# Moving the first product's operands to the same places modulo 256 bytes as the second product's

## The chip, the cores and the metric

One core of a Trainium2 chip runs the kernel. The metric is the device time of one execution in microseconds (us). Three runs of the kernel before gave 1517.08, 1517.21 and 1517.23 us. SBUF, the on-chip memory, has 128 partitions; each tile takes the same byte range in every partition, and "place" below means the address within a partition.

## The reference

Four batches of 12480 tokens of width 128 go through an attention that passes through 32 inducing points, and then all 49920 tokens go through a two-layer network of inner width 2048:

```python
h = mab(I, x)                       # I: 32 inducing vectors, softmax over the 12480 tokens
y = mab(x, h)                       # each token attends to the 32 rows of h
def mab(q, kv):
    s = scale * (q @ kv.transpose(0, 2, 1))
    a = np.exp(s - s.max(-1, keepdims=True))
    a /= a.sum(-1, keepdims=True) + 1e-09
    return a @ kv
t = y @ w_in                        # (49920, 128) @ (128, 2048)
out = (t * sigmoid(1.702 * t)) @ w_out
```

The results are float32. The two weight matrices arrive as 64-bit floats and are decoded on the chip.

## The kernel before

The attention's last product and the first layer are joined: `w_in` is multiplied by `h` ahead of time, so that a block of 512 tokens needs, in place of its 128 attention outputs, only its 32 attention weights. Each operand is split into a rounded part and a remainder, and the parts are stacked on the 128 partitions. Per block of 512 tokens there are 16 chunks of 128 inner columns. They are handled two at a time, as a *group*.

- `hidden(i)` issues the two **first products** of group i: weights `hw` (128x128), moving columns `st` (512 tokens), result in a two-bank PSUM tile `ph`. Two such tiles take turns. (A shorter last block of each batch uses the tile `left` in place of `st`.)
- `first(i)` then lets ScalarE make `g` (the gated value) from `ph`, ScalarE or VectorE make `hi` (its rounded part), and VectorE make `lo = g - hi`.
- `second(i, c)` issues three **second products** for each chunk c: weights `wl` with moving `hi`, weights `wh` with moving `lo`, weights `wh` with moving `hi`. The 48 of one block add up in one PSUM tile `pso`, of which two take turns; ScalarE copies it out to `ob` at the end.

So a group is eight matmuls of 512 columns. TensorE's order is written out in advance: the loop at the end of the kernel puts in the two first products of a later group when its own cost model says that a `ph` tile is free, else the next second products. Matmuls of the next batch's attention (`pa`, from `xt`, `xn`, `indT_sb`, `hT`) are put in between by the same means. Each engine then runs its list in order, held by semaphores.

Both operands of a rounded matmul are read from SBUF. `by_lines` makes the 512 moving columns be read as four passes; in each pass 4 neighbouring columns (16 bytes) are taken out of every 16 (64 bytes):

```python
LINES = (4, 4)
ASIDE = 4
def by_lines(ap):
    return ap.rearrange("p (n s i) -> p s n i", s=LINES[0], i=LINES[1])
```

The weights of a matmul are 128 neighbouring float32 (512 bytes). `aside` places `hw`, `wh` and `wl` 4 elements (16 bytes) behind the start of their tile. Where each tile starts follows from the order in which the pools are opened and from the sizes of the small tiles in the pools between them (`SMALL` says which small tile goes to which pool).

Of the kernel before, what the change touches and what calls it, by code (L numbers as in the profile page):

```python
# [9 lines left out]
F32 = mybir.dt.float32  # L10
# [10 lines left out]
P = 128  # L21
# [44 lines left out]
FB = 6  # L66
LINES = (4, 4)
ASIDE = 4
SMALL = {"m2": "psm1", "less": "psm2", "rs2": "psm4", "row": "psm4", "mx": "psm4", "den": "psm5", "rs": "psm5", "sm": "psm6"}
WINDOW = 100.0  # L70
CHAIN = 200.0
CALM = 0
# [179 lines left out]
def set_attention_then_moe(ctx: ExitStack, tc, xT, x, indT, w_in, w_out, outT):  # L252
# [75 lines left out]
    const = ctx.enter_context(tc.tile_pool(name="const", bufs=1))  # L328
# [3 lines left out]
    pools = {}  # L332

    def pool_of(name, bufs=1):
        pools[name] = ctx.enter_context(tc.tile_pool(name=name, bufs=bufs))
        return pools[name]
# [10 lines left out]
    pool_of("psm5", 2)  # L347
    pool_of("pwl")
    pool_of("psm6", 3)
    pools["psm5"].tile([P, 8], F32, tag="aside", name="aside", bufs=1)  # L350

    def small(shape, tag, name, **k):
        return pools[SMALL.get(tag, "psm3")].tile(shape, F32, tag=tag, name=name, **k)

# [21 lines left out]
    rep2 = rep.rearrange("p g m -> p (g m)")  # L376
    mine = const.tile([P, M], F32, name="mine")
    dve.tensor_scalar(mine, rep[:, 0, :], -scale, None, op0=ALU.mult)
    ones = const.tile([1, 2], F32, name="ones")
    one, warm = ones[:, 0:1], ones[:, 1:2]  # L380
    dve.memset(one, 1.0)
    act.activation(warm, one, AF.Exp)
# [1235 lines left out]
```

## Time and profile before

| | before |
|---|---|
| median of 3 runs | 1517.21 us |
| time of the profiled execution | 1517.26 us |
| its span, first to last instruction | 1515.5 us |
| TensorE matmuls busy | 1507.8 us (99%) |
| ScalarE busy | 1343.5 us (89%) |
| VectorE busy | 1300.5 us (86%) |
[...]

The span is what the trace covers; 1.8 us of the execution's time lie around it. "PE" is TensorE's matmuls and "PEld" its weight loads, "DVE" VectorE, "ACT" ScalarE. Matmuls overlap in the pipeline, so a matmul's shown duration is longer than the time from its start to the next one's start, which this document calls a *step*.

### The profile page before, as it was taken

To read this page: it belongs to the slowest core of one execution; us is meant where nothing else is said; L and a number is where in the kernel's file an instruction comes from. 1 tells how busy PE (TensorE), PEld (TensorE's weight loads), DVE (VectorE), ACT (ScalarE), POOL (GpSimd) and SP (SyncE) were. 2 spreads that over 40 slices of the span, in tenths; PEclk is the share of its full clock that TensorE was granted. 3 is DMA by queue.
4 is the path that set the end of the run, shared out by engine and by line. 5 is a ranking of instruction groups with operands and counts; after the bars stand their busy time and mean duration, and the time that the engine had idled before them with its cause. 6 is when DMAs were issued, how large, how long until landed. Compare 5 with 4: busy or idle time off the path is not lost.

```text
span 1515.5 us, 21743 instructions
## 1 busy us (share of the span) xinstructions
PE 1507.8 (99%) x7736; PEld 1226.8 (81%) x7736; DVE 1300.5 (86%) x1512; ACT 1343.5 (89%) x1549; POOL 0.7 (0%) x6
## 2 busy tenths in 40 slices
PE   9999999999999999999999999999999999999999
PEld 6588878887888888887887888888788888888888
DVE  7988888889888887889889888778988898888996
ACT  4899999998999888899999898989899998988884
POOL 0000000000000000000000000000000000000000
PEclk9999999999999999999999999999999999999999
DMA  8210167713051115933123110871301101101100
GB/s 339 64 62 23 42 217 125 200 56 105 30 211 43 34 32 99 187 105 103 44 98 136 41 49 15 160 205 55 100 23 40 49 25 39 49 22 42 49 24 23
DMA packets 83849, 127.53 MB, mean 84 GB/s; under 512 B 12320, under 2 KB 50848, under 8 KB 77856
## 3 DMA queue, kind: packets, MB, share of 16 engines
q1 hardware_dynamic: 83600, 126.05, 29.5%
q8 instruction: 63, 1.03, 0.3%
q14 instruction: 42, 0.34, 0.1%
q10 hardware_dynamic: 144, 0.10, 0.0%
HBM read 72.11 MB, written 25.56 MB: 64 GB/s over the span
## 4 chain that ended last, share of the span: by engine, by line
PE 98%; DVE 1%; DMA 1%; ACT 0%; issue 0%; SPq 0%
PE pso L185 69%; PE ph L185 24%; PE pa L185 4%; PE h L185 0%; PE spun L1299 0%; DMA xt<-in_xT 0%; ACT g L185 0%; DMA hw<-tl 0%; DVE e L185 0%; DVE sm L185 0%; ACT s L185 0%; DVE m L185 0%; DVE two L185 0%; DVE aT L185 0%; DVE hw L185 0%
## 5 line engine op out<-in xcount | busy, mean ns | idle before, releaser
L185 DVE TENSOR_TENSOR lo<-g,hi 128x1024 fp32r<-128x1024 f32 x776 | 937.7, 1216 | 117.8 <-ACT hi L185 104.9
L185 ACT ACTIVATE g<-ph 128x1024 f32<-128x1024 f32 (+1 forms) x784 | 814.6, 1045 | 135.3 <-PE ph L185 68.0
L185 PE MATMUL pso<-hi,wh 128*128 128x512 f32 (+1 forms) x1552 | 593.8, 383 | 0.0
L185 PE MATMUL pso<-hi,wl 128*128 128x512 f32 (+1 forms) x1552 | 590.2, 380 | 0.0
L185 PE MATMUL pso<-lo,wh 128*128 128x512 f32 (+1 forms) x1552 | 589.6, 380 | 0.0
L185 ACT ACTIVATE hi<-ph 128x1024 fp32r<-128x1024 f32 (+1 forms) x493 | 515.0, 1045 | 0.0
L185 PE MATMUL ph<-st,hw 128*128 128x512 f32 x1536 | 477.2, 394 | 1.3 <-ACT g L185 0.9
L185 PEld LDWEIGHTS ph<-st,hw 128*128 128x128 f32 x1536 | 284.7, 187 | 72.2 <-issue 9.6
L185 PEld LDWEIGHTS pso<-hi,wl 128*128 128x128 f32 x1552 | 291.0, 187 | 59.7 <-issue 2.5
L185 PEld LDWEIGHTS pso<-lo,wh 128*128 128x128 f32 x1552 | 291.0, 187 | 57.6
L185 PEld LDWEIGHTS pso<-hi,wh 128*128 128x128 f32 x1552 | 291.2, 188 | 49.9
L185 DVE CAST hi<-g 128x1024 fp32r<-128x1024 f32 (+1 forms) x283 | 193.6, 684 | 71.4 <-ACT g L185 71.0
L185 ACT COPY ob<-pso 128x512 f32<-128x512 f32 (+1 forms) x98 | 60.6, 619 | 9.9 <-PE pso L185 9.7
L185 ACT ACT_TABLE_LOAD x26 | 33.4, 1283 | 1.2 <-PEq L1608 0.7
L185 PE MATMUL pa<-xt,indT_sb 128*32 128x512 f32 x200 | 24.9, 600 | 0.6 <-DVE aT L185 0.6
L185 ACT ACTIVATE s<-s,nmx 128x512 f32<-128x512 f32 (+1 forms) x27 | 17.8, 660 | 4.2 <-DVE nmx L185 4.2
L185 PE MATMUL pa<-xt,hT 128*32 128x512 f32 (+1 forms) x176 | 21.3, 593 | 0.0
L185 DVE TENSOR_TENSOR e<-e,sm 128x512 f32<-128x512 f32 (+3 forms) x29 | 17.8, 613 | 1.0
L185 DVE TENSOR_REDUCE m<-e 128x16 f32<-128x512 f32 (+2 forms) x28 | 17.3, 618 | 1.0
L185 DVE STREAM_TRANSPOSE aT<-s 128x512 f32<-128x512 f32 (+1 forms) x28 | 17.9, 641 | 0.2
L185 DVE TENSOR_REDUCE sm<-e 128x16 f32<-128x512 f32 (+3 forms) x29 | 17.3, 597 | 0.4 <-ACT e L185 0.4
L185 DVE TENSOR_TENSOR e<-e,m 128x512 f32<-128x512 f32 (+2 forms) x28 | 17.3, 616 | 0.0
(120 smaller groups left out, 356.9 us busy)
## 6 DMA issues: line engine op xcount, KB each, us to landing
xt<-in_xT SPq DMA_DIRECT2D x44, 1024.0 KB, 7.9
out_T<-ob SPq DMA_DIRECT2D x96, 256.0 KB, 2.0
xn<-in_x SPq DMA_DIRECT2D x72, 256.0 KB, 7.3
st<-ahT SPq DMA_DIRECT2D x184, 64.0 KB, 2.0
st<-alT SPq DMA_DIRECT2D x184, 64.0 KB, 2.0
raw<-in_w_in SPq DMA_DIRECT2D x4, 512.0 KB, 10.8
xf<-in_x SPq DMA_DIRECT2D x2, 1024.0 KB, 17.3
raw<-in_w_out SPq DMA_DIRECT2D x4, 512.0 KB, 15.3
```

The source lines that it names most:

```text
L185: return f(*a, **k)
```

## The change

No instruction is added, removed or put elsewhere: the lists of all five engines are the same, row for row. Some small tiles go to other pools and one (`ones`) leaves the pool of constants. Because of that everything between the constants and the pool `psm3` starts 32 bytes lower, and what lies behind it stays.

```diff
-SMALL = {"m2": "psm1", "less": "psm2", "rs2": "psm4", "row": "psm4", "mx": "psm4", "den": "psm5", "rs": "psm5", "sm": "psm6"}
+SMALL = {"m2": "psm1", "less": "psm2", "den": "psm4", "rs": "psm4", "mx1": "psm5", "nmx": "psm5", "rs1": "psm5", "sm": "psm6"}
...
-    pools["psm5"].tile([P, 8], F32, tag="aside", name="aside", bufs=1)
+    pools["psm4"].tile([P, 8], F32, tag="aside", name="aside", bufs=1)
...
-    ones = const.tile([1, 2], F32, name="ones")
+    ones = pools["psm5"].tile([1, 2], F32, tag="ones", name="ones", bufs=1)
```

The places that follow, modulo 256 bytes, are the same for all buffers of a name (a chunk's 128 weights are 512 bytes, so all chunks of a tile share one place):

| matmul | weights before | moving before | weights after | moving after |
|---|---|---|---|---|
| first product `ph<-st,hw` | 48 | 0 | 16 | 224 |
| second `pso<-hi,wl` | 16 | 224 | 16 | 224 |
| second `pso<-lo,wh` | 16 | 224 | 16 | 224 |
| second `pso<-hi,wh` | 16 | 224 | 16 | 224 |

Within each matmul the weights lie 48 bytes ahead of its own moving columns (the columns 208 bytes behind the weights), before and after. What differs is a pair of neighbours: the weights of the *next* matmul are loaded while the columns of this one stream. From a second product into a first one the weights being loaded lie 80 bytes (48 - 224 + 256) ahead of the columns being streamed, from a first into a second one 16 (16 - 0); after the change it is 48 everywhere. `left`, `xt`, `xn`, `aT`, the score tiles and `w_in_all` go down by 32 bytes too, while `indT_sb`, `hT`, `hi`, `lo` and `g` stay.

## Rows read from the trace of the kernel before

**Rows 1.** Page: engines' busy time; the chain that ended last, by engine and line.
```profile
span 1515.5 us, 21743 instructions
PE 1507.8 (99%) x7736; PEld 1226.8 (81%) x7736; DVE 1300.5 (86%) x1512; ACT 1343.5 (89%) x1549; POOL 0.7 (0%) x6
...
PE 98%; DVE 1%; DMA 1%; ACT 0%; issue 0%; SPq 0%
```

**Rows 2.** Groups of TensorE: names, shape, count | busy us, mean ns | idle before.
```profile
L185 PE MATMUL pso<-hi,wh 128*128 128x512 f32 (+1 forms) x1552 | 593.8, 383 | 0.0
L185 PE MATMUL pso<-hi,wl 128*128 128x512 f32 (+1 forms) x1552 | 590.2, 380 | 0.0
L185 PE MATMUL pso<-lo,wh 128*128 128x512 f32 (+1 forms) x1552 | 589.6, 380 | 0.0
L185 PE MATMUL ph<-st,hw 128*128 128x512 f32 x1536 | 477.2, 394 | 1.3 <-ACT g L185 0.9 <-DMA hw<-tl 0.4
```

**Rows 3.** Timeline of TensorE from 1359.72 us: start us, duration us, engine, matmul.
```profile
1359.72 0.38 PE L185 MATMUL pso<-hi,wl 128*128 128x512 f32 x1
...
1360.82 0.38 PE L185 MATMUL pso<-hi,wh 128*128 128x512 f32 x1
1361.04 0.38 PE L185 MATMUL pso<-hi,wl 128*128 128x512 f32 x1
...
1361.48 0.39 PE L185 MATMUL pso<-hi,wh 128*128 128x512 f32 x1
1361.71 0.62 PE L185 MATMUL ph<-st,hw 128*128 128x512 f32 x2
1362.17 0.38 PE L185 MATMUL pso<-hi,wl 128*128 128x512 f32 x1
```

**Rows 4.** Timeline of ScalarE around 1361 us.
```profile
1360.59 1.10 ACT L185 ACTIVATE g<-ph 128x1024 f32<-128x1024 f32 x1
1361.49 0.68 ACT L185 COPY ob<-pso 128x512 f32<-128x512 f32 x1
```

**Rows 5.** Timeline of TensorE: first and last of 28 first-product pairs.
```profile
1425.42 0.62 PE L185 MATMUL ph<-st,hw 128*128 128x512 f32 x2
...
1473.66 0.62 PE L185 MATMUL ph<-st,hw 128*128 128x512 f32 x2
```

**Rows 6.** Timeline of TensorE at 96.74 us, four first products in a row.
```profile
96.74 0.39 PE L185 MATMUL pso<-hi,wh 128*128 128x512 f32 x1
96.96 1.07 PE L185 MATMUL ph<-st,hw 128*128 128x512 f32 x4
97.87 0.38 PE L185 MATMUL pso<-hi,wl 128*128 128x512 f32 x1
```

**Rows 7.** Windows of 60 us: busy us of PE, PEld, DVE, ACT, POOL; clock.
```profile
70.00:130.00 60.00, 60.00 (x272) 49.16 (x271) 53.89 (x59) 56.65 (x64) 0.00 (x0) 1.00 0.23 75
...
1210.00:1270.00 60.00, 60.00 (x269) 49.96 (x268) 53.04 (x55) 55.73 (x63) 0.00 (x0) 1.00 0.12 36
1270.00:1330.00 60.00, 60.00 (x270) 50.33 (x269) 52.06 (x55) 52.66 (x59) 0.00 (x0) 1.00 0.12 36
...
sum 1440.00, PE 1440.00 PEld 1182.71 DVE 1243.77 ACT 1297.05 POOL 0.00; mean PE 60.00 PEld 49.28 DVE 51.82 ACT 54.04 POOL 0.00
```

**Rows 8.** Waits of ScalarE: us in total, times, longest.
```profile
ACT g L185 <- PE ph L185: 68.0, 103, 2.3
```

**Rows 9.** Groups of TensorE: the attention's float32 matmuls with 512 columns.
```profile
L185 PE MATMUL pa<-xt,indT_sb 128*32 128x512 f32 x200 | 24.9, 600 | 0.6 <-DVE aT L185 0.6
L185 PE MATMUL pa<-xt,hT 128*32 128x512 f32 (+1 forms) x176 | 21.3, 593 | 0.0
```

**Rows 10.** Page, DMA issues: size, median us from issue to landing.
```profile
st<-ahT SPq DMA_DIRECT2D x184, 64.0 KB, 2.0
```

**Rows 11.** Timeline of TensorE from 1362.61 us.
```profile
1362.61 0.38 PE L185 MATMUL pso<-hi,wh 128*128 128x512 f32 x1
1362.83 0.62 PE L185 MATMUL ph<-st,hw 128*128 128x512 f32 x2
1363.29 0.39 PE L185 MATMUL pso<-hi,wl 128*128 128x512 f32 x1
1363.52 0.39 PE L185 MATMUL pso<-lo,wh 128*128 128x512 f32 x1
1363.75 0.38 PE L185 MATMUL pso<-hi,wh 128*128 128x512 f32 x1
1363.97 0.38 PE L185 MATMUL pso<-hi,wl 128*128 128x512 f32 x1
```

## Prediction

> **What bounds the kernel now.** I read the page first. TensorE's matmuls are busy for 1507.8 of a span of 1515.5 us, and the chain that ended last runs through TensorE for 98% of the span [rows 1]. So the time is, nearly, the sum of TensorE's steps (a step is the time from one matmul's start to the next one's). The execution's own 1517.26 us is that span and 1.8 us around it, and it lies 0.05 us above the median of the three runs, so I count against 1517.2. A difference of 0.2%, about 3 us, is what a measurement here can tell from no change.
>
> Next come the groups of TensorE's lines. Four matmul forms make up nearly all of its work, and three of them have mean durations of 380 to 383 ns, while the first product `ph` has 394 [rows 2]. Idle time before all of them is 1.3 us, so waits on other engines are not what makes `ph` longer. Durations are modelled and overlap, so I went on to starts, in the timeline. From 1359.72 to 1361.48 us, eight steps between second products take 1.76 us, 0.220 us each. Then the steps around the pair of first products: from 1361.48 to 1362.17 us, three steps take 0.69 us instead of 0.66 [rows 3]. [...] The timeline rounds to 10 ns, so I take a long stretch: 28 pairs of first products, evenly spaced, stand between 1425.42 and 1473.66 us, which is 27 groups of eight matmuls in 48.24 us, 1.787 us for one [rows 5]. Eight steps of 0.220 us would be 1.760. **The excess is 26.7 ns for each group**, and it sits around the first products. That is what a change to the first products' operands can reach.
>
> **Is it the places?** In front of a first product the weights being loaded lie 80 bytes ahead of the columns that stream, behind it 16, and in all steps between second products 48. The slow steps are where this differs. Two other things differ there: `ph` is another PSUM bank, and it starts a new sum. Rows 3 hold a counterexample for both. The last product of a block is the one at 1360.82 us (the copy `ob<-pso` of that block follows on ScalarE at 1361.49, behind the `g` that holds ScalarE until then [rows 4]), so the one at 1361.04 us begins a new sum in the other bank, and its step is 0.22 like the rest. One thing speaks against the relative place alone: the step within the pair has 48 bytes as well, yet it is not free. Three steps with 30 ns over leave about 10 for each [rows 3]. I take it as the tail of the disturbance that the step before began, for two reasons. First, disturbances here outlast their cause: around 1362.83 us the two steps behind a pair, from 1363.29 to 1363.75 us, take 0.23 each, with the places of the quick steps, and then 0.22 returns [rows 11]. Second, four first products in a row at 96.96 us reach the next second product after 0.91 us, 0.2275 each, less than the 0.23 a step of [rows 3] [rows 6]. If it is the absolute place that counts instead, the change answers that too, since 0 and 48 become 224 and 16.
>
> **The change, step by step.**
> 1. Instructions added or removed: none, and no list changes its order. Nothing is moved past a queue, and no wait is added.
> 2. Steps around the first products: all eight steps of a group get the same places, those of the 0.220 us steps. Bounds: nothing, if places don't matter, and 26.7 ns a group if each step comes down to 0.220. I take the upper bound, because the quick step is seen with exactly these places and the differences other than places are contradicted by [rows 3]. There are 1536 first products [rows 2], so 768 pairs: 768 x 26.7 ns = 20.5 us at most. Not all pairs stand alone between second products. In the first stage some wait for ScalarE, and others have attention matmuls as neighbours. I take off a tenth for these (a choice): 18.5 us.
> 3. What ScalarE gives back: a `ph` tile comes free when ScalarE is done with it, and TensorE then needs it soon. Over 24 windows ScalarE is busy 1297 of 1440 us, 90% [rows 7]. With groups of 1.760 us the same work would be 1.787 / 1.760 x 90% = 91.4%. So on the whole it follows, and it waits for TensorE's `ph` 103 times, 68 us in all [rows 8]; a quicker TensorE shortens these waits. But in 11 of the 24 windows it is busy for over 55.2 us (the first is 70 to 130 us with 56.65, the last 1210 to 1270 with 55.73), where 1270 to 1330 has 52.66 [rows 7]. Even 56.65 becomes only 57.5 of 60, but inside a window there are runs in which it has no pause, and there its pace holds. Bounds: nothing lost, or all of the saving in these 11 windows, 11/24 x 18.5 = 8.5 us. I take a third, 2.8 us, nearer to nothing, because no window is full and TensorE's present wait for ScalarE before `ph` is 0.9 us [rows 2].
> 4. The attention's float32 matmuls: `xt` and its like move by 32 bytes against `indT_sb` and `hT`. The trace has no such pairing at the new places. There are 376 instructions of these two forms [rows 9], four at a time on four column strips, so 94 steps. If each changes by the 10 ns of the first products' steps, that is 0.9 us either way; I take 0.
> 5. DMA: the stacks are written to 224 instead of 0. They land 2.0 us after issue [rows 10], a block or more ahead of use, and no wait of a matmul for them is shown. Should one take twice as long, 2 us more are still covered; I take 0. The small tiles that change pools are used a few times for each batch, off TensorE's list: 0.
>
> Sum: 1517.2 - 18.5 + 2.8 = **1501.5 us**.
>
> [...]
>
> **Rivals.**
> - *No change.* The excess belongs to the first products as such (their semaphore, the turn from one operand stream to another), not to places. For it: before and after the change each matmul's own weights and columns are 48 bytes apart, and the step within the pair is slow at 48. Against it: the step across banks and sums in [rows 3], and that a step is already slow before the first product starts, while a second product streams (1361.48 to 1361.71 us, 0.23). Time 1517.2.
> - *ScalarE becomes the pace.* All savings in the 11 fuller windows are lost: 1517.2 - 10.0 = 1507.2. For it: 56.65 busy of 60, and two `ph` tiles only. Against it: 68 us of its waits for `ph`.
> - *Slower.* With the same places everywhere nothing shakes the streams out of a bad phase. The steps of 0.23 us in [rows 11] have exactly the places that all steps will have. If that phase lasts, a group is 8 x 0.230 = 1.840 us, 53 ns more than now, and the kernel loses 768 x 53 ns = 41 us: 1558. It decides once more than 2.7 of a group's eight steps stay in it (26.7 ns / 10 ns). Against it: in [rows 11] it ends after two steps, and the runs of steps between second products in [rows 3] have none.
>
> **How the numbers follow.** The forecast gets 0.70, with a range of its own from 1496 (the 20.5 us, nothing given back, and 0.9 us from the attention) to 1505 (a fifth of the excess left, 3.7 us). ScalarE's pace gets 0.12, no change 0.12, the slower phase 0.06. Faster by over 0.2% is 0.70 + 0.12 = 0.82, within 0.2% 0.12, slower 0.06. The range takes in the forecast and ScalarE's rival with some room above it, 1496 to 1512; no change and slower, 0.18 together, are left out.
>
> **What would show it.** In the changed trace the mean of `ph` should come down from 394 toward 381 to 384 and that of `pso<-hi,wh` from 383 toward 381, and an even stretch of 27 groups should take 47.5 us instead of 48.2. If the group still takes 1.787 us, places are not the cause. If it takes 1.760 in even stretches but the time falls by less than 12 us, step 3 was too small: TensorE's wait for `g` before `ph` would grow from 0.9 us, and ScalarE's waits for `ph` shrink below 68. If steps of 0.23 fill stretches between second products, the slower phase is real. Float32 matmuls with means away from 600 and 593, or waits of `ph` for a DMA, would show steps 4 and 5 wrong.

## The result, and the profile after

The changed kernel takes 1500.36 us (median of 5 runs, 1500.09 to 1500.63) against 1517.21; the ratio is 0.9889, 95% interval 0.9875 to 0.9904. 16.85 us went.

The page after, engines' busy time:

```profile
span 1498.6 us, 21743 instructions
PE 1491.7 (100%) x7736; PEld 1228.1 (82%) x7736; DVE 1300.1 (87%) x1512; ACT 1342.6 (90%) x1549; POOL 0.7 (0%) x6
```

VectorE and ScalarE are busy as long as before, within a microsecond; TensorE's busy time fell by 16.1 us [rows 1]. The groups of TensorE's lines after (mean ns behind the busy us):

```profile
L185 PE MATMUL pso<-hi,wl 128*128 128x512 f32 (+1 forms) x1552 | 589.9, 380 | 0.0
L185 PE MATMUL pso<-hi,wh 128*128 128x512 f32 (+1 forms) x1552 | 589.0, 380 | 0.0
L185 PE MATMUL pso<-lo,wh 128*128 128x512 f32 (+1 forms) x1552 | 588.4, 379 | 0.0
L185 PE MATMUL ph<-st,hw 128*128 128x512 f32 x1536 | 464.8, 386 | 1.2 <-ACT g L185 1.1
L185 PE MATMUL pa<-xt,indT_sb 128*32 128x512 f32 x200 | 24.7, 600 | 0.7 <-DMA xt<-in_xT 0.7
L185 PE MATMUL pa<-xt,hT 128*32 128x512 f32 (+1 forms) x176 | 21.3, 593 | 0.0
```

The first product came down from 394 to 386 ns and `pso<-hi,wh`, the one in front of it, from 383 to 380, the level of the others [rows 2]. The prediction expected 381 to 384 for the first product. Of the 1536, 47 last over 400 ns (46 before) and hold the mean up; the others came down from 389.9 to 381.3. The attention's float32 matmuls kept their means [rows 9]. The steps show it directly, in the timeline of TensorE after ("..." stands for lines left out):

```profile
1402.46 0.38 PE L185 MATMUL pso<-lo,wh 128*128 128x512 f32 x1
...
1402.90 0.60 PE L185 MATMUL ph<-st,hw 128*128 128x512 f32 x2
1403.34 0.38 PE L185 MATMUL pso<-hi,wl 128*128 128x512 f32 x1
...
1412.83 0.60 PE L185 MATMUL ph<-st,hw 128*128 128x512 f32 x2
...
1453.31 0.60 PE L185 MATMUL ph<-st,hw 128*128 128x512 f32 x2
```

The four steps from 1402.46 to 1403.34 us, around a pair, take 0.88 us now, 0.220 each (the three around a pair took 0.69 in [rows 3]). From 1412.83 to 1453.31 us there are 23 evenly spaced groups in 40.48 us, 1.760 us each, against 1.787 [rows 5].

### The profile page after: what moved, and what is told of

Same layout as the page of the kernel before. It is cut to its first block, busy times and chain, and to the rows that moved or that the text cites. A ratio compares the mean times of both kernels' runs of the same rounds, so it can differ in the third digit from the quotient of the medians.

```text
span 1498.6 us, 21743 instructions
## 1 busy us (share of the span) xinstructions
PE 1491.7 (100%) x7736; PEld 1228.1 (82%) x7736; DVE 1300.1 (87%) x1512; ACT 1342.6 (90%) x1549; POOL 0.7 (0%) x6
## 4 chain that ended last, share of the span: by engine, by line
PE 96%; DMA 2%; DVE 1%; ACT 1%; issue 0%; SPq 0%; DVEq 0%
PE pso L185 68%; PE ph L185 23%; PE pa L185 4%; DMA xt<-in_xT 2%; ACT g L185 0%; PE h L185 0%; DVE lo L185 0%; DVE e L185 0%; PE spun L1299 0%; DMA hw<-tl 0%; DVE sm L185 0%; ACT L185 0%; SPq L200 0%; ACT hi L185 0%; DVE m L185 0%
## 5 line engine op out<-in xcount | busy, mean ns | idle before, releaser
L185 ACT ACTIVATE g<-ph 128x1024 f32<-128x1024 f32 (+1 forms) x784 | 812.7, 1043 | 119.6 <-PE ph L185 62.1
L185 PE MATMUL ph<-st,hw 128*128 128x512 f32 x1536 | 464.8, 386 | 1.2 <-ACT g L185 1.1
```

What stands on the lines that cost most here:

```text
L185: return f(*a, **k)
```

## The experiments

Each kernel keeps the order of all five engines' lists unless the text says otherwise, and each was timed beside the kernel before (medians of 1517.1 to 1517.3 us). Ratios are against that kernel, with the 95% interval in brackets. "Distance" is how far the weights being loaded lie ahead of the columns being streamed, counted modulo 256 bytes (a way of counting: whether anything repeats there stays open, see the last section).

**One half of the change at a time.** Small tiles are dealt out differently so that only the first products' columns move (to 224), or only their weights (to 16). Against the kernel before:

```diff
 # columns_only  (and bufs=3 for the tile m2)
-SMALL = {"m2": "psm1", "less": "psm2", "rs2": "psm4", "row": "psm4", "mx": "psm4", "den": "psm5", "rs": "psm5", "sm": "psm6"}
+SMALL = {"row": "psm1", "less": "psm1", "mx": "psm2", "m2": "psm3", "nmx": "psm4", "rs1": "psm4", "mx1": "psm4", "rs2": "psm4", "den": "psm5", "rs": "psm5", "sm": "psm6"}
 # weights_only  (of SMALL only this entry)
-... "less": "psm2" ...
+... "less": "psm1" ...
...
-    ones = const.tile([1, 2], F32, name="ones")
+    ones = pools["psm3"].tile([1, 2], F32, tag="ones", name="ones", bufs=1)
```

> The columns of the first products lie at 224 as after the change, their weights at 48 as before; the second products are unchanged. The weights being loaded then lie 80, 80 and 48 bytes ahead of the streaming columns in the three steps around a pair of first products (before 80, 48, 16; after 48, 48, 48). Theory, the distance between the next weights and the streaming columns decides: two of three steps stay slow, 1507 to 1514 us. Rival, the place of the columns alone decides: 1500.4 us, as after the whole change. Rival, the place of the weights alone decides: 1517 us.

Measured: 1523.73 us, ratio 1.0041 (1.0026 to 1.0056). This is slower than before the change, and outside what any of the three theories gave.

> The weights of the first products lie at 16 as after the change, their columns at 0 as before. The distances of the three steps are 48, 16 and 16. Theory, the distance between the next weights and the streaming columns decides: the step into a first product becomes quick, the two others stay slow, 1507 to 1514 us. Rival, the place of the weights alone: 1500.4 us. Rival, the place of the columns alone: 1517 us.

Measured: 1514.28 us, ratio 0.9981 (0.9971 to 0.9990), just above the range that the distance theory gave.

Neither rival holds: the place of one operand alone does not set the time. Counted from the changed kernel, two steps at distance 80 cost 1523.73 - 1500.36 = 23.4 us and two steps at 16 cost 13.9. Half of each, 18.6 us, is near the 16.85 us of the kernel before, which has one of each. So the prices nearly add; my expectations failed because they took 80 and 16 for equally dear. The views round starts to 10 ns, and the traces keep them to 1 ns; single steps below are from the traces. The steps, in TensorE's timeline of weights_only:

```profile
1440.72 0.38 PE L185 MATMUL pso<-hi,wh 128*128 128x512 f32 x1
1440.94 0.61 PE L185 MATMUL ph<-st,hw 128*128 128x512 f32 x2
1441.40 0.38 PE L185 MATMUL pso<-hi,wl 128*128 128x512 f32 x1
```

and of columns_only:

```profile
1440.43 0.39 PE L185 MATMUL pso<-hi,wh 128*128 128x512 f32 x1
1440.66 0.63 PE L185 MATMUL ph<-st,hw 128*128 128x512 f32 x2
1441.13 0.38 PE L185 MATMUL pso<-hi,wl 128*128 128x512 f32 x1
1441.35 0.39 PE L185 MATMUL pso<-lo,wh 128*128 128x512 f32 x1
1441.57 0.38 PE L185 MATMUL pso<-hi,wh 128*128 128x512 f32 x1
1441.80 0.38 PE L185 MATMUL pso<-hi,wl 128*128 128x512 f32 x1
```

In the first, from 1440.72 us, the step at 48 takes 220 ns, the two at 16 take 220 and 232, and the next two, at 48 again, 223 and 225. In the second, from 1440.43 us, the two steps at 80 take 226 and 238 ns, and the next three, all at 48, 229, 221 and 225. In the kernel before, around the pair of [rows 3], the steps at 80, 48 and 16 take 226, 229 and 232. So a step does not show its own distance alone: the first one at 16 has no excess, and steps at 48 behind a bad one are slow. That is the tail which the prediction assumed. In the medians over the 656 pairs that stand between second products, the same steps lie within 1 ns of these.

**The same distance at another place.** Everything 32 bytes lower than after the change, by dealing out small tiles anew, taking two out of the constants' pool and padding. Against the kernel before:

```diff
-SMALL = {"m2": "psm1", "less": "psm2", "rs2": "psm4", "row": "psm4", "mx": "psm4", "den": "psm5", "rs": "psm5", "sm": "psm6"}
+SMALL = {"mx1": "const", "rs2": "const", "m2": "psm1", "less": "psm2", "den": "psm4", "rs": "psm4", "nmx": "psm5", "sm": "psm6", "rs1": "psm6"}
...
-    pools["psm5"].tile([P, 8], F32, tag="aside", name="aside", bufs=1)
+    pools["const"] = const
+    for k in (3, 5):
+        pools[f"psm{k}"].tile([P, 8], F32, tag="aside", name="aside", bufs=1)
...
-    mine = const.tile([P, M], F32, name="mine")
+    mine = pools["psm5"].tile([P, M], F32, tag="mine", name="mine", bufs=1)
...
-    ones = const.tile([1, 2], F32, name="ones")
+    ones = pools["psm4"].tile([1, 2], F32, tag="ones", name="ones", bufs=1)
...
-        sm = small([P, BLK], tag="sm", name="sm")
+        sm = small([P, BLK], tag="sm", name="sm", bufs=2)
```

> All rounded products' weights and columns lie 32 bytes lower than after the change, at 240 and 192; the distance stays 48 everywhere (one small tile has two buffers instead of three). Theory, the distance decides: 1500.4 us, within 2 us. Rival, the place itself decides (224 is a good place for columns, others are not): steps of 0.225 to 0.233 us everywhere, 30 to 80 us more, 1530 to 1580 us.

Measured: 1500.11 us, ratio 0.9885 (0.9870 to 0.9900): as the changed kernel. A shift of both operands by 32 bytes has no price; no other shift was tried.

**Other distances, the same in every step.** The weights start 0, 6 or 8 elements behind the start of their tile instead of 4, or the small tiles are dealt out so that the weights lie 64 or 128 bytes higher. The first kind is against the changed kernel, the second against the kernel before (there `m2` and `sm` also have bufs=3):

```diff
 # distance_32, distance_56, distance_64
-        return t[:, ASIDE:ASIDE + n * WC]
+        return t[:, 8:8 + n * WC]        # distance 64; 0 gives 32, 6 gives 56
...
-SMALL = {"m2": "psm1", "less": "psm2", "rs2": "psm4", "row": "psm4", "mx": "psm4", "den": "psm5", "rs": "psm5", "sm": "psm6"}
 # distance_112
+SMALL = {"mx1": "const", "row": "psm1", "less": "psm2", "nmx": "psm2", "m2": "psm3", "den": "psm4", "rs": "psm4", "sm": "psm5", "rs2": "psm5", "rs1": "psm6", "mx": "psm6"}
 # distance_176
+SMALL = {"mx1": "const", "nmx": "const", "rs1": "psm1", "row": "psm2", "less": "psm2", "m2": "psm3", "den": "psm4", "rs": "psm4", "sm": "psm5", "rs2": "psm5", "mx": "psm6"}
...
-    pools["psm5"].tile([P, 8], F32, tag="aside", name="aside", bufs=1)
+    pools["const"] = const
+    pools["psm3"].tile([P, 8], F32, tag="aside", name="aside", bufs=1)
...
-    ones = const.tile([1, 2], F32, name="ones")
+    ones = pools["psm4"].tile([1, 2], F32, tag="ones", name="ones", bufs=1)
```

> All weights of the rounded products lie 16 bytes higher than after the change, at 32, with the columns at 224: the distance is 64 in every step. Theory, only certain distances are quick, and 16 and 80 are not: steps of 0.225 to 0.233 us throughout, 1530 to 1580 us. Rival, it is the turn from one distance to another that costs, and any distance is quick if it is the same throughout: 1500.4 us, within 2 us.

> All weights of the rounded products lie 64 bytes higher than after the change, at 80, with the columns at 224: the distance is 112 in every step. Theory A, the distance counts modulo 64 bytes, the pitch of the column passes: 1500.4 us, within 2 us. Theory B, it counts modulo 256 bytes: 112 is a distance of its own, and most distances are slow, so 1520 to 1560 us.

> All weights lie 16 bytes lower than after the change, at 0, with the columns at 224: the distance is 32 in every step. Theory, only certain distances are quick: a step at 16 cost about 9 ns over and one at 64 about 8, so 32 should cost something too, 1510 to 1555 us. Rival, 32 lies in the quick range with 48: 1500.4 us, within 2 us.

> All weights lie 8 bytes higher than after the change, at 24: the distance is 56 in every step, between 48 (quick) and 64 (1551 us). Theory, pieces of 16 bytes meet each other and half a piece is as good as the slow side: 1530 to 1551 us. Rival, the cost rises evenly with the distance from 48: about 1525 us. Rival, only the piece in which the weights begin counts: 1500.4 us.

> All weights of the rounded products lie 128 bytes higher than after the change, at 144, with the columns at 224: the distance is 176 in every step, 48 and 128. Theory A, the distance counts modulo 128 bytes: 1500.4 us, within 2 us. Theory B, it counts modulo 256 bytes: a distance of its own, 1510 to 1560 us like 32, 64 and 112.

| distance in every step | us | ratio (95%) | mean ns of `pso<-hi,wl` |
|---|---|---|---|
| 32 | 1536.45 | 1.0128 (1.0113 to 1.0143) | 386 |
| 48 (after) | 1500.36 | 0.9889 (0.9875 to 0.9904) | 380 |
| 48 (all_32_lower) | 1500.11 | 0.9885 (0.9870 to 0.9900) | 380 |
| 56 | 1567.16 | 1.0328 (1.0314 to 1.0342) | 391 |
| 64 | 1551.12 | 1.0217 (1.0202 to 1.0232) | 389 |
| 112 | 1520.91 | 1.0025 (1.0016 to 1.0034) | 384 |
| 176 | 1522.48 | 1.0040 (1.0028 to 1.0051) | 384 |

The ten runs at 176 spread from 1520.23 to 1528.97 us, those at 112 from 1519.17 to 1522.52, so these two medians say less than the others. Sameness alone buys nothing: at 64 the steps of a group are all slow and differ from each other, as TensorE's timeline of distance_64 shows.

```profile
1440.05 0.39 PE L185 MATMUL pso<-lo,wh 128*128 128x512 f32 x1
1440.27 0.39 PE L185 MATMUL pso<-hi,wh 128*128 128x512 f32 x1
1440.50 0.39 PE L185 MATMUL pso<-hi,wl 128*128 128x512 f32 x1
1440.73 0.40 PE L185 MATMUL pso<-lo,wh 128*128 128x512 f32 x1
1440.97 0.39 PE L185 MATMUL pso<-hi,wh 128*128 128x512 f32 x1
```

The four steps there are 227, 231, 231 and 238 ns. And 112 and 176, which are 48 plus 64 and 48 plus 128, are slower than 48: the pattern does not repeat every 64 or 128 bytes. 56 costs more than 64 and more than any theory gave it, so the price doesn't rise evenly either. 32 and 64 fell into the range of the distance theory, 112 and 176 into that of theory B.

By the trace it is the matmuls that get longer, not the weight loads. The page of distance_56:

```profile
PE 1558.9 (100%) x7736; PEld 1228.4 (78%) x7736; DVE 1302.9 (83%) x1512; ACT 1348.1 (86%) x1549; POOL 0.7 (0%) x6
```

Against the changed kernel TensorE's matmuls are busy 67.2 us longer, its weight loads 0.3 us.

**The order in which the columns are read.** The places are those after the change; only `LINES` changes.

```diff
-LINES = (4, 4)
+LINES = (1, 16)      # columns_in_a_row; eight_passes: (8, 4); sixteen_passes: (16, 4)
```

> The places are those after the change, but the 512 columns are read one behind the other instead of in four passes of 16 bytes out of every 64. Theory, the steps' excess comes from two streams that meet in the same piece of memory: columns and weights then move through memory at one pace, a meeting lasts through the whole weight load or never comes, and the steps move clearly, by 10 ns or more each, 1560 us or above, if they meet, and towards 1475 to 1495 us if they never do. Rival, the order in which the columns are read has nothing to do with it: 1500.4 us.

> The places are those after the change, the columns are read in eight passes of 16 bytes out of every 128. Four passes (pitch 64) gave 1500.4 us, sixteen (pitch 256) 1855.9. Theory, memory repeats every 256 bytes and the step depends on how many places modulo 256 the columns visit: two instead of four, so something between, 1520 to 1700 us. Rival, only a pitch of a whole 256 is slow: 1500 us, within 10 us.

> The places are those after the change, but the columns are read in 16 passes of 16 bytes out of every 256. Theory that the distance modulo 256 decides: within one weight load the columns stay at four places modulo 256, the weights pass each of them twice, and the steps change by 5 ns or more each, 1470 or 1530 us or beyond. Rival, any spread reading is as good: 1500.4 us, within 3 us.

Measured: 1577.16 us in a row (1.0396, 1.0379 to 1.0413), 1636.82 with a pitch of 128 bytes (1.0788, 1.0771 to 1.0804) and 1855.93 with a pitch of 256 (1.2234, 1.2216 to 1.2253). The mean of `pso<-hi,wl` is 396, 406 and 445 ns, and all four big groups rise together, here in the lines of sixteen_passes:

```profile
L185 PE MATMUL pso<-hi,wl 128*128 128x512 f32 (+1 forms) x1552 | 689.9, 445 | 0.0
L185 PE MATMUL pso<-hi,wh 128*128 128x512 f32 (+1 forms) x1552 | 688.6, 444 | 0.0
L185 PE MATMUL pso<-lo,wh 128*128 128x512 f32 (+1 forms) x1552 | 688.5, 444 | 0.0
L185 PE MATMUL ph<-st,hw 128*128 128x512 f32 x1536 | 556.4, 449 | 0.9 <-ACT g L185 0.6
```

Same bytes, same products, only the order of the columns differs. All three times fell where the theories put them, in wide ranges. What the theories assume, a memory that repeats every 256 bytes and a pace at which the weight load goes past the columns, no run tests. The rivals that the order has nothing to do with it, or that only a pitch of 256 is slow, fall. The columns' result was written to PSUM in the same changed order, so these three runs alone don't tell reading from writing. And all three have a distance of 48: whether another distance is quick in another order was not tried, so these runs don't show that the order acts through the meeting of weights and columns.

**What is left after the change.** The rule that shares out `hi` between the engines charges ScalarE 200 ns more. This makes a new order of all lists, with 426 instead of 493 `hi` on ScalarE.

```diff
-        if act.t + 165 + 1.667 * n <= max(dve.t, act.t) + 150 + 1.06 * n:
+        if act.t + 365 + 1.667 * n <= max(dve.t, act.t) + 150 + 1.06 * n:
```

> The places are those after the change; the rule that shares out the rounded part hi charges ScalarE 200 ns more, so that 426 instead of 493 of them go to ScalarE and the others to VectorE, and the order follows. Theory, what is left of the slow steps after the change comes from pairs of first products whose ph tile ScalarE frees late, about 90 pairs and 3 to 4 us: with ScalarE some 70 us lighter most of it goes, 1496.5 to 1499 us. Rival, the late pairs have another cause, or VectorE, 46 us heavier, now makes others late: 1500 us or more.

Measured: 1505.74 us, ratio 0.9924 (0.9911 to 0.9936), 5.4 us more than the changed kernel; the expected gain did not come. TensorE's timeline of scalar_lighter shows why it is slower:

```profile
1032.35 0.61 PE L185 MATMUL ph<-st,hw 128*128 128x512 f32 x2
1035.00 0.77 PE L185 MATMUL pso<-hi,wl 128*128 128x512 f32 x1 [2.04 <-DVE tl L185]
1035.57 0.63 PE L185 MATMUL pso<-lo,wh 128*128 128x512 f32 x1
1035.99 0.63 PE L185 MATMUL pso<-hi,wh 128*128 128x512 f32 x1
```

Two such waits for VectorE's `tl` (the changed kernel has none) come to 4.1 us, and behind this one the steps double for a while (last section): from 1035.00 us eight steps take 3.52 us instead of 1.76, another 1.8. The two together are the 5.4 us and a little more. What the experiment was for, the pairs that ScalarE holds up, it leaves open: their number hardly changed (74 against 81, counted as below). A likely reason, not tested, is that the order is planned against ScalarE's work and puts the first products just behind its new end again.

## Why the prediction was right

**What bounds the kernel**: right. TensorE's busy time fell by 16.1 us and the time by 16.85; no other engine's work changed. The granted clock was 1.000 over the whole of both profiled executions, and the steps compared all have 512 columns [rows 3], so neither sets the slow steps apart.

**The places as the cause**: shown. columns_only, weights_only, all_32_lower and the five other distances change nothing but places, and the time follows the distance between the weights and the streaming columns, from 1500 to 1567 us. That it is the *next* matmul's weights is shown by the change itself: a matmul's own weights lie 48 bytes ahead of its own columns before and after. (In the five other distances both change together.) The prediction's arguments against the other PSUM bank and the new sum [rows 3] hold (with the same banks and sums the three steps around the pair at 1402.68 us take 0.220 us each now), and so does its reading of the pair's inner step as a tail. The rival *no change* falls. Between 48 and 56 bytes of distance alone lie 66.8 us, and by the pages of the two runs it is the matmuls that got longer (67.2 us of busy time), not the weight loads (0.3). By what path the distance acts on the matmuls, no run shows.

**Step 2, the gain**: of the ceiling of 20.5 us 16.85 came, and in even stretches it is there in full, 1.760 us a group. Since both kernels have the same lists, each step after can be set against the same step before. Of the 768 pairs, 656 stand between second products; the 112 others, with all the rest of the kernel, gained 1.5 us instead of the 3.0 that 26.7 ns for each would give. That is the loss for which the prediction took off a tenth, 2.05 us: a choice, and near in size.

**Step 3, what ScalarE gives back**: 2.8 us was near the 2.5 found below, but that is luck: it was a third of a bound, chosen, and the form was another. I had expected waits of TensorE or runs at ScalarE's pace. The wait before `ph` grew only from 0.9 to 1.1 us, and ScalarE's own waits for `ph` fell from 68.0 [rows 8] to 62.1:

```profile
ACT g L185 <- PE ph L185: 62.1, 93, 2.3
```

What happens is seen in the timeline of all engines of the changed kernel:

```profile
1402.68 0.38 PE L185 MATMUL pso<-hi,wh 128*128 128x512 f32 x1
1402.68 0.41 PEld L185 LDWEIGHTS ph<-st,hw 128*128 128x128 f32 x2
...
1408.03 1.02 ACT L185 ACTIVATE hi<-ph 128x1024 fp32r<-128x1024 f32 x1
...
1409.06 0.39 PE L185 MATMUL pso<-hi,wh 128*128 128x512 f32 x1
1409.09 0.38 PEld L185 LDWEIGHTS ph<-st,hw 128*128 128x128 f32 x2
1409.28 0.62 PE L185 MATMUL ph<-st,hw 128*128 128x512 f32 x2
...
1409.74 0.38 PE L185 MATMUL pso<-hi,wl 128*128 128x512 f32 x1
```

ScalarE lets go of the `ph` tile at 1409.05 us. The weights of the first product are loaded from 1409.09, 30 ns into the running matmul, where the other load shown, at 1402.68, starts together with its matmul. No matmul waits, but the three steps from 1409.06 to 1409.74 take 0.68 us instead of 0.66, at the very places that are quick elsewhere. To 1 ns the three steps are 225, 229 and 233, nearly those that distances of 80, 48 and 16 gave before (226, 229 and 232).

I matched each weight load with its matmul by their order in the trace. Of the 656 pairs between second products, the load of the first one's weights starts within 3 ns of the running matmul in 575: they gained 15.8 us, against 15.4 by the ceiling. In 81 it starts 16 ns or more behind, in each of them within 80 ns of the end of an instruction of ScalarE that reads `ph`. Instead of gaining 2.2 us these lost 0.3, which is 2.5 us short. So 2.5 with late loads and 1.5 with the 112 other pairs, less the 0.4 that the early ones have over, are the 3.6 us that the trace lacks of the ceiling. The prediction took off 4.85 for the two, so its 1501.5 us came out 1.1 too high. ScalarE's part in this is not all new: 34 of the 656 loads were already that late before the change. Lateness and price don't grow together: of the 40 loads that are 35 to 38 ns late, 39 cost 26 or 27 ns over five steps, and the eight that are 60 ns late 20 ns each. That the late load is what slows these steps is read from the trace; no run varied it alone.

**Steps 4 and 5**: right; the float32 matmuls kept their means, and no matmul waited for a stack.

**The rival of a slow phase everywhere** did not come about at 48, where steps return to 0.220, but it is what happens at the other distances: at 64 all eight steps of a group are slow. Its price was of the right size for a distance badly chosen: it gave 1558 us, and 64 and 56 took 1551 and 1567.

## What to carry to other kernels

When a matmul's step is longer than its neighbours' and nothing waits, look at where the *next* matmul's weights lie against the columns that stream now, not only at one matmul's own operands: here 8 bytes of distance were worth 4% and the order of reading the columns up to 24%. Equal places are no merit in themselves; find a distance whose steps are quick, by measuring, and then give it to every matmul that can follow another. Moving small tiles between pools is enough for it, and the lists of the engines stay the same.

## What was not expected of the hardware

- The quick distance was quick only in one of the four read orders tried: 48 bytes with a pitch of 64 gave a steady 0.220 us, while the same 48 with a pitch of 256 took 1855.93 us in all. Why 48 is quick, and over how many bytes the pattern repeats beyond the 128 that distance_176 excludes, stays open.
- Steps behind a weight load that starts some 36 ns late cost as much as a bad distance (27 ns in three steps), although no matmul waits. That they are the same three steps as with the bad distances suggests that what counts is where the two reads stand against each other in time; no run tests that.
- After one of the two waits of some 2.0 us in scalar_lighter the granted clock fell. Its windows (from and to, us; length, PE's busy us and matmuls; granted clock; DMA share and GB/s):

```profile
1030.00:1033.00 3.00, 2.96 (x14) 1.00 0.00 0
1033.00:1035.00 2.00, 0.00 (x1) 1.00 0.47 161
1035.00:1038.00 3.00, 3.00 (x7) 0.51 0.30 73
1038.00:1041.00 3.00, 3.00 (x14) 0.92 0.38 95
```

TensorE was busy for 2.96 of the 3 us until 1033, stood still for two microseconds, and was then granted 0.51 of its full clock over 3 us and 0.92 over the next 3; from 1035.57 us a step took 0.42 us. After the other wait, between 670 and 676 us (3.97 of 6 us busy), the clock stayed at 1.00. Why it fell after the one and not after the other, no run shows.
